# Turning activation tiles through the DMA queue instead of TensorE, in a windowed-attention and mixer kernel

## The chip, the cores and the metric

The kernel runs on one core of a Trainium2 chip. The metric is device time in microseconds (us) of one execution; lower is better. The kernel before took 568.84 us (median of three runs, 568.76 to 569.65).

The engines are named as in the profile: PE is TensorE, DVE is VectorE, ACT is ScalarE, POOL is GpSimd, and SP is SyncE, whose queue issues nearly all transfers.

## The reference, cut to what matters

```
scores = q @ k.T / 8 + bias ; keep = first n_global keys or the last n_local
x  = softmax(scores) @ v                       # 2 x 768 rows, 8 heads x 64 = 512 columns
xn = (x - mean) / sqrt(var + 1e-6) * g_ln      # first mixer layer
x  = x + relu(xn @ w_ch1) @ w_ch2              # 512 -> 2048 -> 512
h  = relu(x.T @ w_tok1) @ w_tok2               # token mixing over 768 rows, per batch
u  = x + h.T
out = u + relu(u @ w_ch1') @ w_ch2'            # 512 -> 1536 -> 512
```

The 1536 rows are twelve tiles T = 0 to 11 of 128 rows, six per batch. Two arrays of activations must be turned (rows to columns) before a product can contract over the 512 columns: the normalised tile `xn` and, after token mixing, the tile `u`, each once per T.

## The kernel before, in words

Products of the mixer run on float16 pairs. A float32 tile is split in a high half (rounded to float16) and a low half (what is left), and a product is three matmuls: high x high, high x low, low x high (`mm3`, lines 372 to 374). So whatever feeds a product is split: ACT writes the high half, then DVE or POOL subtracts it and writes the low half.

The tiles T form four groups of three. Group 0 and 2 are turned into a buffer named `xa`, groups 1 and 3 into `xb`; group 2 reuses the buffer of group 0 when the last product that reads group 0 is done, likewise 3 after 1. The first mixer layer runs as five passes: group 0 with hidden columns 0 and 1 (of four blocks), group 1 the same, then both with block 2, both with block 3, and then groups 2 and 3 together. In that last pass, from its second block on, and in the second channel layer, `mlp_ops` uses a scheme of fewer products with sums of operands (`Factors`, `summands`, tiles `fx`, `sz`, `Q`, `K`, `V`; bank name `chain`). Results of the second product of a layer (`L2`, `L2S`) are added to `x` by DVE at line 872.

Token mixing of batch 0 (T = 0 to 5) is interleaved with the pass of groups 2 and 3, that of batch 1 with the second channel layer of batch 0. Its second product writes `tok`, DVE adds that to `x` (line 1040), and the new tile is turned: T = 0 to 5 into tiles `u`, T = 6 to 11 into `xa` and `xb` again.

Turning, before, is `transpose_ops` (line 558): four matmuls of PE against an identity (line 565) write a PSUM bank, ACT reads the bank and writes the high half (line 358), DVE reads it and writes the low half (line 367). The bank is of pool `k` for `norm` (shared with `chain`) and of pool `t` for `uT` (shared with `L2S`, `T`, `PV` and `tok` of the second product); each pool has two banks.

The order of all instructions is written by a planner (`Plan.order`): every operation has an engine, an assumed duration, a priority from tables of numbers (SLOT, AHEAD, LEAD, DUE and so on), and the planner plays them on a model of the engines. An operation marked `lock` is not started while another locked one of DVE or POOL runs by the model. While group 0 isn't turned, `emit` puts filler matmuls (`keep_busy`, line 106) where the model sees PE idle in its first stretch. SP's queue is in order too: a transfer that waits holds those behind it.

Weights come as 64-bit words: a load into `stg`, ACT makes `fw` (line 727), DVE makes `wf` (line 733), ACT writes the high half (line 749), and POOL (line 752) or DVE (line 755) the low half, of `wa`, `wb` or `t`. Strings such as LOA1 name the engine for each.

Of the kernel before, what the change touches and what calls it, by code (L numbers as in the profile page):

```python
# [17 lines left out]
AF = mybir.ActivationFunctionType  # L18
ALU = mybir.AluOpType
# [549 lines left out]
    plan.op("V", 0.6, prio, l, r=[(b, 0), (*w, "h")], w=[(*w, "l")])  # L569


def xk(T):

    return [("x", T, 0), ("x", T, 1)]


def norm_ops(o, plan, prio, T, grp, i):

    nc = o.nc
    x = o.x[T]  # L580
    st = Buf("st", lambda: o.ln.tile([P, 9], F32, tag="st", name="st", bufs=2))
    xn = Buf("xn", lambda: o.ln.tile([P, C], F32, tag="xn", name="xn", bufs=o.sizes["xn"]))

    def stats():
        nc.vector.bn_stats(out=st.t[:, 0:6], in_=x[:])
        nc.vector.bn_aggr(out=st.t[:, 6:8], in_=st.t[:, 0:6])
        nc.vector.tensor_scalar(out=st.t[:, 8:9], in0=st.t[:, 7:8], scalar1=1e-6, scalar2=None, op0=ALU.add)

    k0 = 4 * T
    op = plan.op  # L590
    op("V", 1.0, prio(k0 + SLOT["st"]), stats, r=xk(T), w=[(st, 0)], get=[st])

# [93 lines left out]
class Weights:  # L686
# [26 lines left out]
    def split(self, src, prio, dst, key, get=(), r=(), after=()):  # L713
        o, nc, op = self.o, self.o.nc, self.plan.op
        wide = o.half and (src[1] == "b" or src[0] == "tok2")
        fine = o.half and not wide
        scale = W3 if fine else W8 if wide and not o.w64 else 1.0
        engs = {(1, "a"): LOA1, (1, "b"): LOB1, (2, "a"): LOA2, (2, "b"): LOB2}.get(src[:2], LOT)
        lo_eng = "V" if scale != 1.0 else engs[src[2]] if o.w64 else "G"
        stg = Buf("stg", lambda: next(o.stg))  # L720
        if o.w64:
            if src in o.staged:
                op("N", max(LOADED[src], HOLD[src[2]]), -9.0 + 0.1 * src[2], lambda: None, w=[(stg, 0)], get=[stg])
            else:
# [24 lines left out]
        op("A", 0.54, prio, lambda: nc.scalar.activation(
            out=dst()[0], in_=shaped(), func=AF.Copy, scale=scale), r=[w, *r], w=[(*key, "h")], get=get, after=after)  # L750
        if lo_eng == "G":
            op("G", 1.26, prio, lambda: nc.gpsimd.tensor_tensor(
                out=dst()[1], in0=shaped(), in1=plain(dst()[0]), op=ALU.subtract), r=[w, (*key, "h"), *r], w=[(*key, "l")], after=after)
        else:
            op("V", 0.6, prio, lambda: nc.vector.scalar_tensor_tensor(
                out=dst()[1], in0=shaped(), scalar=scale, in1=plain(dst()[0]), op0=ALU.mult, op1=ALU.subtract),
               r=[w, (*key, "h"), *r], w=[(*key, "l")], after=after)


def w_view(o, src):  # L760
# [241 lines left out]
def token_ops(o, plan, b, uT, prio):  # L1002
# [27 lines left out]
    for i in range(NT):  # L1030
# [16 lines left out]
AHEAD = {'s': 12.69, 'k': 30.71, 'q': -33.13, 'v': 33.57}  # L1050
STORE, RELOAD = 9.55, -14.48

LOA1 = 'GVGVGVVVGGGVGVVG'
LOB1 = 'GGGVGVGVVGGVGGVG'
LOA2 = 'VGGGGVVGVVVV'
LOB2 = 'GVVVVGVGVGVG'
LOT = 'VVG'
MK0, MK1, MK2 = 'AAVAVVAV', 'AVVAVAAA', 'VVVAAVVA'
HEAD0 = -200.0
MASK2 = 0.1  # L1060
BUSY = 10, 3
HOLD = [-37.47, 19.06, -39.64]
FIRST = [("k", 0), ("q", 0), ("k", 1), ("q", 1), ("v", 0), (1, "a", 0), ("v", 1), (1, "a", 1), ("k", 2), ("q", 2), (1, "a", 2), ("v", 2)]
LOADED = {("k", 0): 0.0, ("q", 0): 0.0, ("k", 1): 0.0, ("q", 1): 0.6, ("v", 0): 1.5, (1, "a", 0): 3.2, ("v", 1): 4.1,
          (1, "a", 1): 5.8, ("k", 2): 6.7, ("q", 2): 7.5, (1, "a", 2): 9.2, ("v", 2): 10.1}
SPLIT = 6
PVE, VCAST = 'AAAVAA', 'AV'
EVX = 'AAAAVVVAAAAV'
# [7 lines left out]
BANKS = {'L1': 'm', 'L2': 'm', 'L2S': 't', 'norm': 'k', 'chain': 'k', 'uT': 't', 'S': 's', 'T': 't', 'PV': 't', 'tok1': 's', 'tok2': 't'}  # L1076
PSUMS = ('m', 's', 't', 'k')
WIDE = {'hid': 5, 'wa': 5, 'wb': 5, 'stg': 3, 'fw': 2, 'wf': 2, 'st': 2, 'xn': 1, 'mn': 3, 'sum': 3, 'ex': 3, 'pt': 2, 'ph': 2, 'pl': 2, 'ao': 2, 'xz': 3, 'sx': 8, 'raw0': 1, 'raw1': 1, 'xa': 1, 'xb': 1, 'm': 2, 'k': 2, 's': 2, 't': 2}
SIZES = {**WIDE, 'hid': 12, 'wa': 8, 'wb': 8, 'wf': 4, 'fw': 3, 'stg': 4, 'xn': 2, 'xz': 3, 'sz': 4}


def store(o, T):
# [24 lines left out]
def rest(o, ctx, attn, fast):  # L1107
# [40 lines left out]
        plan.busy = lambda n: keep_busy(o, idle.t, n)  # L1148
        plan.op("A", 0.55, HEAD0 + 7.5, lambda: [nc.scalar.memzero(y[:]) for y in o.more_fw], w=[("zeros",)])
    attn.ops(o, plan, prio)  # L1150
    last = len(plan.ops)
    for T in range(NTT):
        norm_ops(o, plan, lambda k, T=T: prio(T, k), T, g[of[T][0]], of[T][1])
    if fast:
        plan.op("T", 0.0, 0.0, lambda: setattr(plan, "busy", lambda n: None), r=[(g[0], 1, "h")], w=[(idle, 0)])
    grp = lambda i: (G[i], lambda: g[i].t, gkeys(g[i], n=len(G[i])))
# [41 lines left out]
    for T in range(NTT):  # L1198
        i, j = divmod(T, 3)
        sl = slice(j * P, (j + 1) * P)  # L1200
        if i < 2:
            uT[T] = (lambda i=i, sl=sl: (o.u[i][:, 0, :, sl], o.u[i][:, 1, :, sl])), ("u", i, j), (), ()
        else:
            uT[T] = (lambda i=i, sl=sl: (u[i].t[:, 0, :, sl], u[i].t[:, 1, :, sl])), (u[i], j), ([u[i]] if j == 0 else []), ()
    token_ops(o, plan, 0, uT, lambda n: t - TOK0 + n * (TOK0 - 8) / 26)
    if not fast:
        token_ops(o, plan, 1, uT, lambda n: t - 1 + n * 0.7)
# [38 lines left out]
HEAD = 95.26
DUE = [45.62, 34.37, 67.54, -5.33]
EARLY = [22.25, -19.91, -2.29, -26.75]
LEAD = -124.75
EVAC = 17.45  # L1250
TOK1 = -39.91
TOKW, TOK0 = 143.17, 142.91
# [199 lines left out]
```

## Time and profile before

| what | value |
|---|---|
| median of three runs | 568.84 us |
| profiled execution, its own time | 568.15 us |
| its span | 566.3 us |
| PE busy | 551.8 us (97%) |
| DVE busy | 425.0 us (75%) |
| ACT busy | 333.7 us (59%) |
| POOL busy | 141.3 us (25%) |
| DMA traffic | 80.79 MB, mean 143 GB/s |

The span runs from the first to the last instruction of the program; the device time of the same execution is 1.85 us longer. A busy share is the time in which an engine had an instruction in work; for PE, whose matmuls overlap, the distance between the starts of two matmuls says more than the length of one. The table of stages gives for each stretch the busy time of each engine, the granted TensorE clock (1.00 is full speed) and the share of the sixteen DMA engines.

### The profile page before, as it was taken

To read this page: it belongs to the slowest core of one execution; us is meant where nothing else is said; L and a number is where in the kernel's file an instruction comes from. 1 tells how busy PE (TensorE), PEld (TensorE's weight loads), DVE (VectorE), ACT (ScalarE), POOL (GpSimd) and SP (SyncE) were. 2 spreads that over 40 slices of the span, in tenths; PEclk is the share of its full clock that TensorE was granted. 3 is DMA by queue.
4 is the path that set the end of the run, shared out by engine and by line. 5 is a ranking of instruction groups with operands and counts; after the bars stand their busy time and mean duration, and the time that the engine had idled before them with its cause. 6 is when DMAs were issued, how large, how long until landed. Compare 5 with 4: busy or idle time off the path is not lost.

```text
span 566.3 us, 9485 instructions
## 1 busy us (share of the span) xinstructions
PE 551.8 (97%) x3347; PEld 319.3 (56%) x3347; DVE 425.0 (75%) x939; ACT 333.7 (59%) x750; POOL 141.3 (25%) x153
## 2 busy tenths in 40 slices
PE   8989999999999999999999999998999999999995
PEld 6867767555555765555555555554554555555542
DVE  7888999773766667998867889989858976555431
ACT  6998679783744656557664745767735564534210
POOL 2223345440011223623201142233006122110000
PEclk9999999999999999999999999999899999999999
DMA  8777978887668313027423421473303132302012
GB/s 263 222 242 232 295 220 244 271 274 254 208 211 285 96 34 102 4 70 223 134 76 112 131 74 57 170 247 129 115 12 111 38 130 94 131 0 75 1 39 79
DMA packets 62251, 80.79 MB, mean 143 GB/s; under 512 B 21492, under 2 KB 35828, under 8 KB 62196
## 3 DMA queue, kind: packets, MB, share of 16 engines
q1 hardware_dynamic: 62194, 80.11, 43.9%
q8 instruction: 28, 0.46, 0.3%
q14 instruction: 27, 0.22, 0.1%
q10 hardware_dynamic: 2, 0.00, 0.0%
HBM read 61.87 MB, written 17.83 MB: 141 GB/s over the span
## 4 chain that ended last, share of the span: by engine, by line
PE 75%; DVE 15%; ACT 4%; DMA 2%; issue 2%; POOL 1%; SPq 0%; ACTq 0%; POOLq 0%; DVEq 0%
PE L L372 10%; PE L L374 10%; PE L L373 10%; PE L2S L373 7%; PE L2S L372 7%; PE L2S L374 7%; PE S L453 3%; PE chain L372 3%; PE chain L373 3%; PE T L479 3%; PE chain L374 3%; PE PV L484 3%; DVE x L872 2%; DVE wf L733 2%; DVE Q L806 1%
## 5 line engine op out<-in xcount | busy, mean ns | idle before, releaser
L372 PE MATMUL L2S<-wb,h 128*128 128x512 f16 x228 | 86.4, 379 | 0.0
L373 PE MATMUL L2S<-wb,h 128*128 128x512 f16 x228 | 86.4, 379 | 0.0
L374 PE MATMUL L2S<-wb,h 128*128 128x512 f16 x228 | 86.4, 379 | 0.0
L872 DVE SCALAR_TENSOR_TENSOR x<-L2S,x 128x512 f32<-128x512 f32 x57 | 39.1, 687 | 51.1 <-PE L2S L374 51.0
L727 ACT ACTIVATE fw<-stg 128x512 f16<-128x512 bf16 x62 | 47.6, 778 | 15.5 <-DMA stg<-in_moe_w_ch_dram 8.3
L374 PEld LDWEIGHTS <-h 128*128 128x128 f16 x336 | 32.9, 98 | 39.7
L806 POOL TENSOR_TENSOR Q<-wa 128x512 f32<-128x512 f16 x18 | 26.5, 1471 | 110.0 <-issue 65.2
L372 PEld LDWEIGHTS <-h 128*128 128x128 f16 x336 | 32.9, 98 | 36.7 <-issue 1.0
L373 PEld LDWEIGHTS <-h 128*128 128x128 f16 x336 | 32.9, 98 | 35.6
L474 ACT ACTIVATE ex<-ex,mn 128x256 f32<-128x256 f32 (+1 forms) x96 | 41.0, 483 | 8.6 <-DVE mn L469 8.5
L733 DVE SCALAR_TENSOR_TENSOR wf<-stg,fw 128x512 uint32<-128x512 uint32 x62 | 44.3, 726 | 1.0 <-ACT fw L727 0.8
L372 PE MATMUL L<-wb,h 128*128 128x512 f16 x108 | 41.0, 379 | 0.0
L374 PE MATMUL L<-wb,h 128*128 128x512 f16 x108 | 40.9, 379 | 0.0
L373 PE MATMUL L<-wb,h 128*128 128x512 f16 x108 | 40.9, 379 | 0.0
L372 PEld LDWEIGHTS <-wa 128*128 128x128 f16 x268 | 26.3, 98 | 18.8 <-issue 2.0
L373 PEld LDWEIGHTS <-wa 128*128 128x128 f16 x268 | 26.2, 98 | 17.7 <-issue 0.9
L374 PEld LDWEIGHTS <-wa 128*128 128x128 f16 x268 | 26.2, 98 | 17.3
L364 DVE SCALAR_TENSOR_TENSOR h<-L,h 128x384 f16<-128x384 f32 x40 | 22.1, 551 | 18.0 <-ACT h L358 17.9
L358 ACT ACTIVATE h<-L 128x384 f16<-128x384 f32 x40 | 19.5, 488 | 26.4 <-PE L L374 26.0
L372 PE MATMUL L<-xa,wa 128*128 128x384 f16 x104 | 33.9, 326 | 0.1
L374 PE MATMUL L<-xa,wa 128*128 128x384 f16 x104 | 33.9, 326 | 0.0
L373 PE MATMUL L<-xa,wa 128*128 128x384 f16 x104 | 33.9, 326 | 0.0
(241 smaller groups left out, 1412.1 us busy)
## 6 DMA issues: line engine op xcount, KB each, us to landing
stg<-in_moe_w_ch_dram SPq DMA_DIRECT2D x56, 512.0 KB, 4.7
wa<-scr_1a SPq DMA_DIRECT2D x24, 256.0 KB, 3.7
wb<-scr_1b SPq DMA_DIRECT2D x24, 256.0 KB, 3.7
scr_1a<-wa SPq DMA_DIRECT2D x16, 256.0 KB, 5.0
scr_1b<-wb SPq DMA_DIRECT2D x16, 256.0 KB, 3.3
K<-in_k_dram SPq DMA_DIRECT2D x12, 256.0 KB, 3.4
Q<-in_q_dram SPq DMA_DIRECT2D x12, 256.0 KB, 4.2
V<-in_v_dram SPq DMA_DIRECT2D x12, 256.0 KB, 3.8
```

The source lines that it names most:

```text
L358: nc.scalar.activation(out=hi(), in_=src(), func=AF.Relu if relu else AF.Copy)
L364: nc.vector.scalar_tensor_tensor(out=lo(), in0=src(), scalar=0.0, in1=plain(hi()), op0=ALU.max, op1=ALU.subtract)
L372: nc.tensor.matmul(ps, ah, bh, start=first, stop=False, **k)
L373: nc.tensor.matmul(ps, ah, bl, start=False, stop=False, **k)
L374: nc.tensor.matmul(ps, al, bh, start=False, stop=last, **k)
L453: nc.tensor.matmul(bs[j].t[:, i, :w], o.Q[r, qs, p + i, :], o.K[r, slots, p + i, :], start=True, stop=True)
L474: nc.scalar.activation(out=ex.t[:, j, :w], in_=ex.t[:, j, :w], func=AF.Exp, bias=mn.t[:, h:h + 1], scale=-1.0)
L479: nc.tensor.transpose(bt.t[:, j, i, :], ex.t[:, j, i * P:(i + 1) * P], o.ident[:])
L727: op("A", 0.66, prio - 2, lambda: nc.scalar.activation(out=fw.t[:, :, 1], in_=stg.t[:, 4:2049:4].bitcast(BF16), func=AF.Copy, scale=2.0 if ...
L733: op("V", 0.6, prio - 1, lambda: nc.vector.scalar_tensor_tensor(out=raw().bitcast(U32), in0=stg.t.bitcast(U32)[:, 1:1024:2], scalar=13, in ...
L806: op(eng, {"G": 0.1 + n * 0.00227, "V": 0.07 + n * 0.00104}[eng], prio, lambda: e.tensor_tensor(out=out(), in0=a(), in1=b(), op=alu), lock ...
L872: n = op("V", 0.6, prio, lambda: nc.vector.scalar_tensor_tensor(out=x[:], in0=b.t[:], scalar=BACK if o.half else 1.0, in1=x[:], op0=ALU.mu ...
```

## The change

Only the fast float16 branch changes. Where a tile is turned, `turn_ops` stands in place of `transpose_ops`: ACT copies the float32 tile in SBUF to the high half of a new tile `xh`, DVE or POOL (strings NLO and ULO) subtracts and writes the low half beside it, and one DMA on SP's queue (`transpose=True`) turns the 128 x 1024 float16 numbers of both halves into the destination. `xh` and `uh` have two buffers each. The planner is given TURN = 2.5 us for that DMA. The low half of a weight on DVE (line 755) gets `lock=True`. The tables of the planner have other numbers, and some engine strings differ. The operations of the norm tiles now also stand ahead of the point at which the attention's buffers are given up (`last`), since they use its pool.

```diff
+def turn_ops(o, plan, prio, pool, tag, lo_eng, src, r, dst, w, get=()):
+    nc, op = o.nc, plan.op
+    y = Buf(tag, lambda: pool().tile([P, 2, C], F16, tag=tag, name="xh", bufs=o.sizes[tag]))
+    op("A", 0.52, prio, lambda: nc.scalar.activation(out=y.t[:, 0], in_=src(), func=AF.Copy), r=r, w=[(y, "h")], get=[y])
+    e = {"V": nc.vector, "G": nc.gpsimd}[lo_eng]
+    op(lo_eng, {"V": 0.6, "G": 1.26}[lo_eng], prio, lambda: e.tensor_tensor(out=y.t[:, 1], in0=src(), in1=y.t[:, 0], op=ALU.subtract),
+       r=[*r, (y, "h")], w=[(y, "l")], lock=True)
+    op("S", TURN, prio, lambda: nc.sync.dma_start(dst().rearrange("p s k n -> p (s k) n"), y.t[:].rearrange("p s c -> p (s c)"), transpose=True),
+       r=[(y, "h"), (y, "l")], w=[(*w, "h"), (*w, "l")], get=get)
...
+    if o.half:
+        turn_ops(o, plan, prio(k0 + SLOT["tr"]), lambda: ln, "xh", NLO[T], lambda: xn.t[:], [(xn, 0)], lambda: grp.t[:, :, :, sl],
+                 (grp, i), [grp] if i == 0 else [])
+        return
     transpose_ops(o, plan, prio(k0 + SLOT["tr"]), "norm", lambda: xn.t, [(xn, 0)], lambda: (grp.t[:, 0, :, sl], grp.t[:, 1, :, sl]),
...
-               r=[w, (*key, "h"), *r], w=[(*key, "l")], after=after)
+               r=[w, (*key, "h"), *r], w=[(*key, "l")], after=after, lock=True)
...
+        if o.half:
+            turn_ops(o, plan, prio(14 + 2 * i) - (1 - b) * UP, lambda: o.tk, "uh", ULO[T], lambda T=T: o.x[T][:], [*xk(T), ("tk",), *r], dst, key, get)
+            continue
...
-LOT = 'VVG'
+LOT = 'VGG'
+NLO, ULO = 'GGVGGGGGVVGV', 'VGVVVGVGGVVG'
+TURN = 2.5
+UP = 19.85
...
-FE, SE = 'VGGVVVVGVVVV', 'VGVVGVVV'
+FE, SE = 'VVGVGGGGVVGG', 'VGVVVVGV'
```

Counted in the fast branch, the changed program has 96 fewer transposing matmuls (48 `norm`, 48 `uT`), 16 more fillers on PE (51 in place of 35 of `L<-x`), 30 fewer instructions on DVE, 3 fewer on ACT, 32 more on POOL, and 24 more transfers on SP's queue. The other PE instructions are the same in number.

Three places show the order. The first is PE in the head of the program, from the second half of the products with V of T = 2 to the first product of the mixer (`L<-xa`), before:

```order
L484 MATMUL PV<-V,pt 128x65 x8
L479 MATMUL T<-ident,ex 128x128 x4
L453 MATMUL S<-K,Q 128x256 x4
L479 MATMUL T<-ident,ex 128x128 x4
L484 MATMUL PV<-V,pt 128x65 x8
L479 MATMUL T<-ident,ex 128x128 x4
L565 MATMUL norm<-ident,xn 128x128 x4
L479 MATMUL T<-ident,ex 128x128 x4
L453 MATMUL S<-K,Q 128x256 x4
L484 MATMUL PV<-V,pt 128x65 x8
L372 LDWEIGHTS wa
L372 MATMUL L_766<-xa,wa 128x384
```

The same place now:

```order
L484 MATMUL PV<-V,pt 128x65 x8
L479 MATMUL T<-ident,ex 128x128 x4
L453 MATMUL S<-K,Q 128x256 x4
L479 MATMUL T<-ident,ex 128x128 x4
L484 MATMUL PV<-V,pt 128x65 x8
L479 MATMUL T<-ident,ex 128x128 x4
L453 MATMUL S<-K,Q 128x256 x4
L479 MATMUL T<-ident,ex 128x128 x4
L484 MATMUL PV<-V,pt 128x65 x8
L479 MATMUL T<-ident,ex 128x128 x4
L453 MATMUL S<-K,Q 128x256 x4
L479 MATMUL T<-ident,ex 128x128 x4
```

The turn of T = 2 (`norm`) is gone from PE, and one more step of the attention (`S`) with two more `T` stands ahead of the first `L<-xa`, which follows directly on the last row. A row of `S` or `PV` with x4 or x8 is eight or sixteen matmuls in the trace, since a float32 one is recorded twice there.

The second place is SP's queue in the head, with the first transfer that turns a tile (T = 0) and what stands behind it, now:

```order
L580 DMA_TRANSPOSE xa<-xh 128x8x128
L537 DMA V<-in_v_dram 32x8x64
L158 DMA V<-in_v_dram 128x8x64
L535 DMA K<-in_k_dram 128x4x32
L160 DMA K<-in_k_dram 128x512
L160 DMA Q<-in_q_dram 128x512
L725 DMA scr_1a_583<-wa 128x1024
L580 DMA_TRANSPOSE xa<-xh 128x8x128
```

Loads of the next attention tiles are queued behind each turn; before, no such transfer stood between them.

The third place is DVE at the start of the second token product of batch 1 (`z<-tok`, then `x<-tok`), before:

```order
L364 SCALAR_TENSOR_TENSOR z<-tok_4409,z 128x512
L364 SCALAR_TENSOR_TENSOR z<-tok_4410,z 128x512
L806 TENSOR_TENSOR Q<-Q 128x256
L733 SCALAR_TENSOR_TENSOR wf<-stg,fw_62 128x512
L755 SCALAR_TENSOR_TENSOR wa<-wf,wa 128x512
L733 SCALAR_TENSOR_TENSOR wf<-stg,fw_63 128x512
L872 SCALAR_TENSOR_TENSOR x_65<-L2S,x_65 128x512
```

The same place now:

```order
L364 SCALAR_TENSOR_TENSOR z<-tok_4483,z 128x512
L364 SCALAR_TENSOR_TENSOR z<-tok_4484,z 128x512
L823 TENSOR_TENSOR Q<-wa 128x512
L772 SCALAR_TENSOR_TENSOR wa<-wf,wa 128x512
L750 SCALAR_TENSOR_TENSOR wf<-stg_203,fw_204 128x512
L889 SCALAR_TENSOR_TENSOR x_68<-L2S,x_68 128x512
```

Between `z` and the operation that empties an `L2S` bank stood four operations, now three.

## Rows read from the trace of the kernel before

**Rows 1.** The page: busy us of each engine, share, instructions; granted clock by slices.

```profile
PE 551.8 (97%) x3347; PEld 319.3 (56%) x3347; DVE 425.0 (75%) x939; ACT 333.7 (59%) x750; POOL 141.3 (25%) x153
...
PEclk9999999999999999999999999999899999999999
```

**Rows 2.** Chain that ended last: start us, us until the next piece, what.

```profile
13.38 0.55 PE L L106 x5
...
20.30 1.06 PE S L453 x8
...
21.95 1.85 PE PV L484 x16
23.81 0.44 PE norm L565 x4
...
28.84 0.44 PE T L479 x4
...
400.64 0.87 PE uT L565 x8
...
403.46 0.22 PE tok L372
```

**Rows 3.** Groups of PE by line and form: busy us, mean ns; idle before.

```profile
L565 PE MATMUL uT<-ident,x 128*128 128x128 f32 x48 | 7.0, 273 | 0.0
L565 PE MATMUL norm<-ident,xn 128*128 128x128 f32 x48 | 6.9, 273 | 0.0
```

**Rows 4.** PE in time order, head: start us, us, instruction; idle before it, releaser.

```profile
31.60 1.90 PE L484 MATMUL PV<-V,pt 128*128 128x65 f32 x16
...
38.53 1.11 PE L484 MATMUL PV<-V,pt 128*128 128x65 f32 x8 [1.22 <-ACT pt L515]
...
44.11 0.33 PE L372 MATMUL L<-xa,wa 128*128 128x384 f16 x1
...
46.06 0.60 PE L479 MATMUL T<-ident,ex 128*128 128x128 f32 x4
```

**Rows 5.** POOL and DVE in time order: T = 2 from normalised to turned.

```profile
38.08 1.34 POOL L607 TENSOR_TENSOR xn<-xn,gB 128x512 f32<-128x512 f32 x1 [0.93 <-ACT xn L600]
...
41.63 0.69 DVE L367 TENSOR_TENSOR xa<-norm,xa 128x512 f16<-128x512 f32 x1
```

**Rows 6.** DMA issues on the page: KB each, median us from issue to landing.

```profile
wa<-scr_1a SPq DMA_DIRECT2D x24, 256.0 KB, 3.7
...
stg<-in_moe_w_tok_dram SPq DMA_DIRECT2D x6, 512.0 KB, 6.2
...
vb<-vb SPq DMA_DIRECT2D x4, 97.5 KB, 2.2
```

**Rows 7.** Stages: us; PE, PEld, DVE, ACT, POOL busy; PEclk, DMA share, GB/s.

```profile
0.00:100.00 100.00, 94.87 (x732) 71.47 (x733) 87.32 (x303) 80.68 (x184) 34.24 (x64) 1.00 0.80 244
393.00:396.30 3.30, 1.10 (x6) 0.39 (x4) 3.30 (x6) 1.43 (x3) 1.04 (x1) 1.00 0.49 171
396.30:400.00 3.70, 3.39 (x10) 1.29 (x10) 3.02 (x6) 1.39 (x3) 0.00 (x0) 0.54 0.42 147
```

**Rows 8.** All engines in time order around PE's longest wait.

```profile
392.01 1.28 DVE L364 SCALAR_TENSOR_TENSOR z<-tok,z 128x512 f16<-128x512 f32 x2
...
393.76 1.04 POOL L806 TENSOR_TENSOR Q<-Q 128x256 f32<-128x256 f32 x1 [4.83 <-DVE Q L806]
394.14 1.21 DVE L755 SCALAR_TENSOR_TENSOR wa<-wf,wa 128x512 f16<-128x512 f32 x1
...
395.88 0.68 DVE L872 SCALAR_TENSOR_TENSOR x<-L2S,x 128x512 f32<-128x512 f32 x1
...
396.61 0.59 PE L372 MATMUL tok<-z,t 128*128 128x512 f16 x1 [2.50 <-DVE x L872]
...
397.84 0.63 PE L372 MATMUL tok<-z,t 128*128 128x512 f16 x1
```

**Rows 9.** One tile's instructions, `wf`: ns shortest, median, longest; first and last start.

```profile
L755 DVE SCALAR_TENSOR_TENSOR wa<-wf,wa x28: 679/691/1646, 21.3 to 396.8; 128x512 f16<-128x512 f32 x28
```

More of the change, by code (lines that the diff above doesn't have):

```diff
@@ L580, in norm_ops @@
     x = o.x[T]
-    st = Buf("st", lambda: o.ln.tile([P, 9], F32, tag="st", name="st", bufs=2))
-    xn = Buf("xn", lambda: o.ln.tile([P, C], F32, tag="xn", name="xn", bufs=o.sizes["xn"]))
+    ln = o.sm if o.half else o.ln
+    st = Buf("st", lambda: ln.tile([P, 9], F32, tag="st", name="st", bufs=2))
+    xn = Buf("xn", lambda: ln.tile([P, C], F32, tag="xn", name="xn", bufs=o.sizes["xn"]))
     def stats():
@@ L1044, in token_ops @@
         dst, key, get, r = uT[T]
+        if o.half:
+            turn_ops(o, plan, prio(14 + 2 * i) - (1 - b) * UP, lambda: o.tk, "uh", ULO[T], lambda T=T: o.x[T][:], [*xk(T), ("tk",), *r], dst, key, get)
+            continue
         transpose_ops(o, plan, prio(14 + 2 * i), "uT", lambda T=T: o.x[T][:], [*xk(T), ("tk",), *r], dst, key, get)
[L1050 to L1056, printed above, removed]
-LOT = 'VVG'
-MK0, MK1, MK2 = 'AAVAVVAV', 'AVVAVAAA', 'VVVAAVVA'
+AHEAD = {'s': -8.81, 'k': 53.46, 'q': -8.16, 'v': 42.47}
+STORE, RELOAD = 53.17, 7.48
+LOA1 = 'GVGGVVVVVGGVVGVV'
+LOB1 = 'GGGGVGVGVGVVGVVV'
+LOA2 = 'GGGVVVVVVGVG'
+LOB2 = 'VVVVVVGVVVGV'
+LOT = 'VGG'
+NLO, ULO = 'GGVGGGGGVVGV', 'VGVVVGVGGVVG'
+TURN = 2.5
+UP = 19.85
+MK0, MK1, MK2 = 'VVVVAAAA', 'VAVVAAAA', 'AVVVAVAA'
 HEAD0 = -200.0
-MASK2 = 0.1
+MASK2 = -121.51
 BUSY = 10, 3
-HOLD = [-37.47, 19.06, -39.64]
+HOLD = [-39.73, 27.18, 27.27]
 FIRST = [("k", 0), ("q", 0), ("k", 1), ("q", 1), ("v", 0), (1, "a", 0), ("v", 1), (1, "a", 1), ("k", 2), ("q", 2), (1, "a", 2), ("v", 2)]
@@ L1066 @@
 SPLIT = 6
-PVE, VCAST = 'AAAVAA', 'AV'
-EVX = 'AAAAVVVAAAAV'
+PVE, VCAST = 'AAAAVV', 'VA'
+EVX = 'AAVAAVVVVAAV'
 QKC, PVC = 0.266, 0.224
-SLOT = {'gk': -57.12, 'exp': 54.15, 'T': -29.6, 'PV': 0.2, 'inv': -1.8, 'st': 27.26, 'xn': 4.52, 'tr': 4.36}
+SLOT = {'gk': -69.67, 'exp': 60.81, 'T': -40.62, 'PV': -12.2, 'inv': 18.38, 'st': 39.04, 'xn': 13.67, 'tr': 37.13}
 NACT = range(0, 4)
@@ L1078 @@
 WIDE = {'hid': 5, 'wa': 5, 'wb': 5, 'stg': 3, 'fw': 2, 'wf': 2, 'st': 2, 'xn': 1, 'mn': 3, 'sum': 3, 'ex': 3, 'pt': 2, 'ph': 2, 'pl': 2, 'ao': 2, 'xz': 3, 'sx': 8, 'raw0': 1, 'raw1': 1, 'xa': 1, 'xb': 1, 'm': 2, 'k': 2, 's': 2, 't': 2}
-SIZES = {**WIDE, 'hid': 12, 'wa': 8, 'wb': 8, 'wf': 4, 'fw': 3, 'stg': 4, 'xn': 2, 'xz': 3, 'sz': 4}
+SIZES = {**WIDE, 'hid': 12, 'wa': 8, 'wb': 8, 'wf': 4, 'fw': 3, 'stg': 4, 'xn': 2, 'xh': 2, 'uh': 2, 'xz': 3, 'sz': 4}
 def store(o, T):
@@ L1150, in rest @@
     attn.ops(o, plan, prio)
-    last = len(plan.ops)
     for T in range(NTT):
         norm_ops(o, plan, lambda k, T=T: prio(T, k), T, g[of[T][0]], of[T][1])
+    last = len(plan.ops)
     if fast:
@@ L1201, in rest @@
         if i < 2:
-            uT[T] = (lambda i=i, sl=sl: (o.u[i][:, 0, :, sl], o.u[i][:, 1, :, sl])), ("u", i, j), (), ()
+            dst, key, get = (lambda i=i, sl=sl: o.u[i][:, :, :, sl]), ("u", i, j), ()
         else:
-            uT[T] = (lambda i=i, sl=sl: (u[i].t[:, 0, :, sl], u[i].t[:, 1, :, sl])), (u[i], j), ([u[i]] if j == 0 else []), ()
+            dst, key, get = (lambda i=i, sl=sl: u[i].t[:, :, :, sl]), (u[i], j), ([u[i]] if j == 0 else [])
+        uT[T] = (dst if fast else lambda dst=dst: (dst()[:, 0], dst()[:, 1])), key, get, ()
     token_ops(o, plan, 0, uT, lambda n: t - TOK0 + n * (TOK0 - 8) / 26)
@@ L1242 @@
 BLOCKS2 = [[(c, (0, 1)) for c in range(3)]] * 2
-LEADS, FLEAD = -62.8, 212.9
-F2LEAD = [-38.18, -45.25]
-FE, SE = 'VGGVVVVGVVVV', 'VGVVGVVV'
[L1246 to L1252, printed above, removed]
+LEADS, FLEAD = -12.39, 152.38
+F2LEAD = [-40.38, -38.53]
+FE, SE = 'VVGVGGGGVVGG', 'VGVVVVGV'
+HEAD = 85.06
+DUE = [36.2, 20.0, 77.7, 9.05]
+EARLY = [6.29, -8.69, 7.57, -14.12]
+LEAD = -208.54
+EVAC = 35.43
+TOK1 = 41.27
+TOKW, TOK0 = 191.94, 141.69
 SLOW = dict(SLOT={'gk': -30.97, 'exp': 16.12, 'T': -15.37, 'PV': -13.48, 'inv': 9.01, 'st': 17.62, 'xn': 12.62, 'tr': 1.7}, HEAD=107.54, DUE=[32.9, 21.07, 45.09, 4.38], EARLY=[-15.89, -16.66, 3.92, -16.37], LEAD=21.63, EVAC=3.31,
```

## The prediction

> **What bounds the kernel now.** I read the page first: PE is busy for 551.8 of 566.3 us, DVE for 75% [rows 1]. A busy PE is not by itself a bound, so the second view is the chain that ended last, whose times are from start to start: four transposing matmuls take 0.44 us, a 512-column matmul 0.22, five fillers 0.55, all one behind the other with no gap [rows 2]. The reader is to see that PE runs at its own pace for almost the whole span, and that what is taken off PE comes off the time, unless a wait takes its place. Third, the waits: PE's longest is 2.50 us, before the second `tok` product of batch 1, for a DVE operation; right behind it the granted clock is 0.54 over 3.7 us, at 1.00 before, so the slower of the two levels (1.2 GHz in place of 2.4) for most of that stretch [rows 7, 8]. It is the one slice short of a 9 in the page's clock row, and shorter waits, as that of 1.22 us in the head, left it at 9 [rows 1, 4]. Last, the stage of the first 100 us: PE 94.9, DVE 87.3, ACT 80.7, DMA engines 0.80 [rows 7]. Everything is nearly full there, and it is where a new wait would hurt.
>
> **The change part by part.** The sum is made against the profiled execution's own 568.15 us, which is 0.69 below the median of 568.84; differences are taken over to the median unchanged.
>
> *Turns off PE.* 24 turns of four matmuls (48 `norm` and 48 `uT` [rows 3]), each four worth 0.44 us: 24 x 0.44 = 10.6, by the eight of 0.87 us 12 x 0.87 = 10.4 [rows 2]. I take 10.5. All of it is on the path as long as PE is the bound. -10.5.
>
> *Fillers.* 16 more of 0.11 us [rows 2]: 1.76. They stand where the planner expects PE idle in the head; if PE would wait there anyhow they are free. From 0 to 1.76; I take +1.7, since with PE on the path they delay what follows.
>
> *What ACT, DVE and POOL do in place of it.* ACT has 3 instructions fewer, DVE 30 fewer, POOL 32 more. POOL is busy for 25% of the span [rows 1], so it has room; DVE gets lighter. No cost; and the gain stands only in the item on the wait below.
>
> *The transfer that turns a tile.* The trace before has none. It moves 256 KB from SBUF to SBUF. Nearest rows, from issue to landing: a 97.5 KB copy inside SBUF 2.2 us, a 256 KB reload 3.7, a 512 KB load 6.2 [rows 6]. For the low end 2.2, for the high end twice the slowest row, 12.4, because no row excludes that a turn in eight blocks is slow; I take the row of the same size, 3.7 (L below).
> Where does L count? First the head, T = 2. Before, its `PV` ends at 33.50, `xn` at 39.42, the turned tile stands at 42.32 and the first `L<-xa` starts at 44.11, so PE came last, not the tile [rows 4, 5]. After the same `PV`, PE now has six `T` (0.44), three `S` (1.06) and two `PV` (1.85): 9.5 us; before four `T`, one `norm`, two `S` and two `PV`: 8.0, while 10.6 passed, so 2.6 went in waits such as that of 1.22 [rows 2, 4]. The tile needs 5.9 us to `xn`, then a copy and a subtraction at about 0.7 each (as the subtraction before [rows 5]) with some queueing, 2.1 together, then L: 8.0 + L. PE is there after 9.5 (no waits) to 12.1 (the same waits). At L = 3.7 the tile comes at 11.7: a wait from 0 to 2.2; at 6.2, from 2.1 to 4.7. I take +0.8. The 1.5 us of attention that now stand ahead of the first product are not lost.
> Second, the hand-over of `xa` to group 2 and of `xb` to group 3, where the destination is only free after the last product that reads the old group. In the new order PE has, between the last `L<-xa` of group 0 and the first of group 2, 48 matmuls of 384 columns (twelve take 1.95, so 0.163 each [rows 4]), 36 of 512 at 0.216 and some small ones: 16.9 us; for `xb`, 48 and 36 without the small ones: 15.6. The third tile of a group must wait for a buffer of `xh`: two turns in a row and 1.6 us between, 2L + 1.6, so 9.0 at 3.7 and 14.0 at 6.2. Hidden; it begins to cost at L = 7. Third, token mixing: between its last product and the first that reads the turned tiles stand 22.8 us (batch 0) and 29.3 (batch 1), counted in the same way, and no L up to 12.4 gets through that alone. On SP's queue loads of Q, K, V stand behind each turn, as behind a store of weights before; the planner puts the turn where its source is due. +0.8 for all of this.
>
> *The wait at 396 us.* DVE ends `z` at 393.29 and empties the `L2S` bank only at 396.56, with four operations between; one of them, `wa`, took 1.21 where its shortest is 0.68, beside a POOL operation that ran from 393.76 to 394.80 [rows 8, 9]. That form is the one that the planner now keeps apart from POOL's. In the new order three operations stand there, 3 x 0.68 and 0.68 for the emptying: the bank is free 2.7 us behind `z`. PE first has one `tok` product, 6 x 0.216, and now also six 384-column matmuls, 0.98: 2.3. So the wait goes from 2.5 to about 0.5, and the slow stretch, six `tok` matmuls and some more at double length, goes with it: of 3.7 us at 0.54, 3.7 x 0.46 = 1.7 us are lost there [rows 7, 8]. From 0 (DVE comes late again) to -4.2; I take -2.0 - 1.7 = -3.7.
>
> Sum: -10.5 + 1.7 + 0.8 - 3.7 = -11.7, and 568.84 - 11.7 = 557.1 us.
>
> A rule of the Trainium skill speaks against the change: "VectorE: DVE Perf Modes", Rules for kernel authors, says to turn 128x128 on TensorE if a result in PSUM is acceptable and by the DMA crossbar otherwise; its table in The three transpose paths gives 390 ns for the one and 1309 ns for the other. Here four turns of PE took 0.44 us from start to start [rows 2], below that page's figure; eight blocks one behind another at its DMA figure would be an estimate of L of 10.5 us, and the sum would be that of the slow rival below. Another page, "Advanced Engine Details and Errata", X-Bar Transpose (TRN2), has such transfers as fast as others, and by that the sum stands. No row here decides between them.
>
> **The rivals.**
> *A wait takes the place.* The wait at 396 moves and doesn't go (3.7 is not gained), and about 2 us of new ones come in, in the order that all tables changed: 557.1 + 3.7 + 2 = 563. For it: DVE is full around 396 [rows 7], and the head has 2.6 us of such waits. Against: DVE has less to do.
> *The turns are slow, and it gets slower.* One mechanism: L decides over the head (8.0 + L against 10.8, the middle of PE's two times) and over the two hand-overs (2L + 1.6 against 16.9 and 15.6). Beyond L = 8 these cost (L - 2.8) + (2L - 15.3) + (2L - 14) = 5L - 32.1; the gain of 12.5 without the 0.8 is eaten at L = 8.9. At L = 10 they cost 17.9, and the time is 568.84 - 12.5 + 17.9 = 574. For it: the DMA engines are at 0.80 in the head [rows 7], where six of the turns stand. Against: no transfer of 256 KB on the page lands later than in 6.
> *It doesn't do what it says.* PE's turns lay in time that was idle anyhow. Then only the other terms stay, with the cover they lose: 568. Against: the turns start without idle time before them [rows 3].
>
> **How the numbers follow.** Forecast 0.55 (its own range 554 to 561: fillers free and the wait wholly gone at the low end, nothing of the wait gained at the high one); a wait in its place 0.22; slow turns 0.13; no effect 0.05; still faster, below 554, because a lighter DVE also shortens the head's waits, 0.05. The range 552.5 to 566 leaves out the slow turns and part of the rest. A measurement of this kernel can tell 0.2% (1.1 us) from no change. Faster: 0.55 + 0.22 + 0.05 = 0.82; same 0.05; slower 0.13.
>
> **What would show it.** PE's busy time about 9 us lower, no `norm` and `uT`, and DVE below 425 us. The landing of the turns between 2.2 and 6.2 us. The first `L<-xa` between 43 and 48 us. No slice of the clock row below 9 near 390. No wait of PE over 1 us at the first product of group 2 or 3. It is wrong if a turn lands later than 9 us, if PE waits for `xa` or `xb`, or if PE's idle time grows by what its busy time falls.

## The result and the profile after

The changed kernel takes 554.67 us (median of four runs, 554.48 to 554.81); the kernel before took 568.80 beside it. The ratio is 0.9749 [0.9732, 0.9766], a gain of 14.1 us where 11.7 were forecast. The profiled execution took 554.65 us with a span of 552.9. Measured again, beside the last experiments (c1), the ratio was 0.9777 [0.9751, 0.9803], a gain of 12.5.

The page of the changed kernel, in the form of [rows 1]: busy time, share and instructions of each engine, then the granted clock.

```profile
PE 543.2 (98%) x3267; PEld 310.7 (56%) x3267; DVE 408.9 (74%) x909; ACT 334.9 (61%) x747; POOL 178.0 (32%) x185
...
PEclk9999999999999999999999999999999999999998
```

PE is busy for 8.6 us less and idle for 9.7 us (552.9 - 543.2) in place of 14.5 (566.3 - 551.8), so 4.8 less: together the 13.4 us by which the span fell. The slice below 9 near 396 us is gone (the 8 of the last slice lies at the end, where PE has no work left). Where the idle time went is seen by stages. First the kernel before, with the columns of [rows 7] (the stage 0 to 100 stands there):

```profile
200.00:300.00 100.00, 99.28 (x583) 55.08 (x582) 81.55 (x152) 62.56 (x147) 29.32 (x25) 1.00 0.29 90
300.00:400.00 100.00, 97.50 (x509) 50.12 (x507) 89.31 (x153) 61.12 (x131) 27.27 (x20) 0.98 0.39 135
```

And the changed kernel, the same stages, the head and a stretch within it:

```profile
0.00:100.00 100.00, 96.52 (x723) 71.87 (x724) 80.97 (x286) 78.41 (x176) 41.78 (x70) 0.98 0.82 229
40.50:43.90 3.40, 3.40 (x16) 2.56 (x16) 2.46 (x6) 2.85 (x6) 0.14 (x1) 0.50 0.72 230
200.00:300.00 100.00, 100.00 (x533) 51.86 (x532) 72.88 (x126) 61.64 (x144) 35.65 (x31) 1.00 0.52 135
300.00:400.00 100.00, 100.00 (x529) 51.61 (x528) 88.96 (x153) 63.71 (x133) 34.80 (x29) 1.00 0.43 130
```

PE is never idle from 200 to 400 us now: 0.72 + 2.50 = 3.2 us of idle time are gone there, and 1.65 in the first 100 us (94.87 to 96.52), where DVE fell from 87.3 to 81.0. The clock is not at 1.00 all the way: in the profiled execution a stretch at 0.50 (the lower of the two levels) lies at 40.5 us, as long as the one that was at 396. The idle time of the first 100 us is not steady either: the second profile of the same kernel (c1) has no such stretch there and is 0.3 us above the kernel before, not 1.65.

```profile
0.00:100.00 100.00, 95.19 (x718) 70.42 (x719) 80.41 (x286) 77.65 (x175) 41.20 (x69) 1.00 0.84 229
```

The turns themselves, all instructions of the line that issues them: duration on SP's queue in ns (shortest, median, longest), first and last start, and the time from issue to landing in us.

```profile
L580 SPq DMA_TRANSPOSE xa<-xh x9: 1232/1283/1445, 23.1 to 412.5; - x9
L580 SPq DMA_TRANSPOSE xb<-xh x9: 1232/1238/1289, 54.4 to 428.4; - x9
L580 SPq DMA_TRANSPOSE u<-xh x6: 1233/1238/1260, 267.3 to 320.7; - x6
...
DMA to landing us min/median/max: 3.0/3.2/6.2
```

A turn holds SP's queue for 1.24 us and lands after 3.2 us; the prediction had taken 3.7. In the head, in order of time (start, us, engine, line; idle time before and its releaser):

```profile
39.37 1.27 POOL L620 TENSOR_TENSOR xn<-xn,gB 128x512 f32<-128x512 f32 x1 [0.93 <-ACT xn L613]
...
39.74 0.84 PE L479 MATMUL T<-ident,ex 128*128 128x128 f32 x4 [0.40 <-ACT ex L474]
...
42.16 1.28 SPq L580 DMA_TRANSPOSE xa<-xh  x1
...
46.21 0.44 PE L479 MATMUL T<-ident,ex 128*128 128x128 f32 x2 [0.44 <-ACT ex L474]
...
48.38 0.33 PE L372 MATMUL L<-xa,wa 128*128 128x384 f16 x1
```

These answer to [rows 4, 5]. The tile of T = 2 stands at about 45.3 (42.16, and 3.1 for the landing of this transfer) and PE starts the first `L<-xa` at 48.38 with no idle time before it: the turn is hidden. Last, the place of [rows 8], now at 398 us:

```profile
398.17 1.27 DVE L364 SCALAR_TENSOR_TENSOR z<-tok,z 128x512 f16<-128x512 f32 x2
...
399.97 0.68 DVE L772 SCALAR_TENSOR_TENSOR wa<-wf,wa 128x512 f16<-128x512 f32 x1
...
401.17 0.68 DVE L889 SCALAR_TENSOR_TENSOR x<-L2S,x 128x512 f32<-128x512 f32 x1
...
402.92 0.38 PE L372 MATMUL tok<-z,t 128*128 128x512 f16 x1
```

`wa` takes 0.68 us where it took 1.21, DVE empties the bank at 401.85, and PE needs it only at 402.92, with no wait.

### The profile page after: what moved, and what is told of

Same layout as the page of the kernel before. It is cut to its first block, busy times and chain, and to the rows that moved or that the text cites. A ratio compares the mean times of both kernels' runs of the same rounds, so it can differ in the third digit from the quotient of the medians.

```text
span 552.9 us, 9384 instructions
## 1 busy us (share of the span) xinstructions
PE 543.2 (98%) x3267; PEld 310.7 (56%) x3267; DVE 408.9 (74%) x909; ACT 334.9 (61%) x747; POOL 178.0 (32%) x185
## 4 chain that ended last, share of the span: by engine, by line
PE 94%; DVE 2%; ACT 2%; issue 1%; POOL 0%; POOLq 0%; ACTq 0%
PE L L372 12%; PE L L374 12%; PE L L373 12%; PE L2S L374 9%; PE L2S L373 9%; PE L2S L372 9%; PE chain L372 4%; PE chain L374 4%; PE chain L373 4%; PE S L453 4%; PE T L479 3%; PE PV L484 2%; PE tok L374 2%; PE tok L372 2%; PE tok L373 2%
## 5 line engine op out<-in xcount | busy, mean ns | idle before, releaser
L744 ACT ACTIVATE fw<-stg 128x512 f16<-128x512 bf16 x62 | 48.0, 776 | 10.5 <-DMA stg<-in_moe_w_ch_dram 7.2
L474 ACT ACTIVATE ex<-ex,mn 128x256 f32<-128x256 f32 (+1 forms) x96 | 41.6, 480 | 14.1 <-DVE mn L469 13.9
L823 POOL TENSOR_TENSOR sz<-Q,sz 128x512 f16<-128x512 f32 x18 | 22.4, 1242 | 84.6 <-ACT sz L915 84.6
L889 DVE SCALAR_TENSOR_TENSOR x<-L,x 128x512 f32<-128x512 f32 x27 | 18.6, 690 | 22.2 <-PE L L374 22.1
L372 PE MATMUL L<-xa,wa 128*128 128x384 f16 x104 | 34.0, 326 | 0.0
L373 PE MATMUL L<-xa,wa 128*128 128x384 f16 x104 | 33.9, 326 | 0.0
```

What stands on the lines that cost most here:

```text
L372: nc.tensor.matmul(ps, ah, bh, start=first, stop=False, **k)
L373: nc.tensor.matmul(ps, ah, bl, start=False, stop=False, **k)
L474: nc.scalar.activation(out=ex.t[:, j, :w], in_=ex.t[:, j, :w], func=AF.Exp, bias=mn.t[:, h:h + 1], scale=-1.0)
L744: op("A", 0.66, prio - 2, lambda: nc.scalar.activation(out=fw.t[:, :, 1], in_=stg.t[:, 4:2049:4].bitcast(BF16), func=AF.Copy, scale=2.0 if ...
L823: op(eng, {"G": 0.1 + n * 0.00227, "V": 0.07 + n * 0.00104}[eng], prio, lambda: e.tensor_tensor(out=out(), in0=a(), in1=b(), op=alu), lock ...
L889: n = op("V", 0.6, prio, lambda: nc.vector.scalar_tensor_tensor(out=x[:], in0=b.t[:], scalar=BACK if o.half else 1.0, in1=x[:], op0=ALU.mu ...
```

## The experiments

Runs of one table ran on the same chip beside the kernel before. Since the time before differs a little from chip to chip, ratios are compared across tables.

**Code, tables and lock apart.** Three edits come together in the change: the turns, the `lock` on a weight's low half, and new numbers in the planner's tables. Four kernels split them.

| run | ratio to before, 95% | median us (before 567.50) |
|---|---|---|
| a1: turns and lock, old tables | 0.9919 [0.9893, 0.9946] | 564.01 |
| a2: lock and new tables, turns on PE | 0.9932 [0.9910, 0.9953] | 563.57 |
| a3: lock alone | 0.9946 [0.9924, 0.9968] | 564.02 |
| a4: all but the lock | 0.9815 [0.9770, 0.9861] | 557.68 |

*a1*, the changed kernel with the tables of before (those of the turns kept; the same for the tables not shown):

```diff
-SLOT = {'gk': -69.67, 'exp': 60.81, 'T': -40.62, 'PV': -12.2, 'inv': 18.38, 'st': 39.04, 'xn': 13.67, 'tr': 37.13}
+SLOT = {'gk': -57.12, 'exp': 54.15, 'T': -29.6, 'PV': 0.2, 'inv': -1.8, 'st': 27.26, 'xn': 4.52, 'tr': 4.36}
...
-LEAD = -208.54
+LEAD = -124.75
```

> The changed code with the planner's tables of numbers of the kernel before (the lock on the weights' low half stays in, since without it the planner finds no order). Theory PE: what the turns take off PE, 10.5 us, comes off the time whatever the tables; with new waits in an order that was not made for them, 558 to 562. Theory order: the new tables bring most of it; then this stays at 565 or more.

*a2*, the kernel before with the lock and the new tables; `norm` is turned on PE, and its `tr` entry is set to that of `xn`:

```diff
-SLOT = {'gk': -57.12, 'exp': 54.15, 'T': -29.6, 'PV': 0.2, 'inv': -1.8, 'st': 27.26, 'xn': 4.52, 'tr': 4.36}
+SLOT = {'gk': -69.67, 'exp': 60.81, 'T': -40.62, 'PV': -12.2, 'inv': 18.38, 'st': 39.04, 'xn': 13.67, 'tr': 13.67}
...
-LEAD = -124.75
+LEAD = -208.54
...
-               r=[w, (*key, "h"), *r], w=[(*key, "l")], after=after)
+               r=[w, (*key, "h"), *r], w=[(*key, "l")], after=after, lock=True)
```

> The code of before with the lock and with the new tables (one number, the place of the turn of a normalised tile, moved earlier, since the planner finds no order with it), turns on PE. Theory PE: 565 to 572, since PE has the same work as before. Theory order: 560 or less.

*a3*, the kernel before with that last line alone:

> The kernel before with the lock alone. If the collision of DVE and POOL makes the 2.5 us wait at 396 us and the half clock behind it, 564.5 to 566; if that wait comes from the order on DVE, 568 to 570.

*a4*, the changed kernel without it:

> The changed kernel without the lock, all else the same. Theory PE: 554.5 to 556.5, as DVE has room; if the lock matters, 558 or more, with a wait of PE for DVE of 2 us or more somewhere from 200 to 430 us.

Taken to the 568.80 us of the result by their ratios, the four are 564.2, 564.9, 565.7 and 558.3 us. So a1 falls between its two theories, a2 just under that of PE, and a3 into the range of the collision; a4 falls into the range in which the lock matters, but without the wait that was named for it (below).

a3: the lock alone gains 0.54%, 3.1 us. Its clock row and two stages:

```profile
PEclk9999999999999999999999999999999999999999
...
200.00:300.00 100.00, 100.00 (x590) 55.77 (x589) 83.01 (x157) 64.19 (x152) 27.59 (x25) 1.00 0.29 90
300.00:400.00 100.00, 100.00 (x536) 52.70 (x535) 86.44 (x156) 63.06 (x137) 25.54 (x20) 1.00 0.39 131
```

Idle time of 2.5 us and the slow stretch are both gone, by one edit of the planner's rules and with every turn still on PE; so are the 0.72 us from 200 to 300, with DVE at 83.01, above the 81.55 of before. But the edit changes the order too. DVE by itself, at the place of [rows 8] in a3:

```profile
388.00 1.29 DVE L364 SCALAR_TENSOR_TENSOR z<-tok,z 128x512 f16<-128x512 f32 x2 [0.64 <-ACT z L360]
389.21 0.42 DVE L806 TENSOR_TENSOR Q<-Q 128x256 f32<-128x256 f32 x1
389.54 0.68 DVE L733 SCALAR_TENSOR_TENSOR wf<-stg,fw 128x512 uint32<-128x512 uint32 x1
390.14 0.69 DVE L872 SCALAR_TENSOR_TENSOR x<-L2S,x 128x512 f32<-128x512 f32 x1
```

Between `z` and the emptying of the bank stand two operations in place of four, and `wa` is not one of them: the bank is free 1.5 us behind `z`, where it was 3.3. So the lock takes the wait away; whether by a shorter `wa` or by the order that it leads to, a3 does not part. And the lock is not needed for it in the new order: in a4, PE waits at this place for 0.29 us.

```profile
405.88 0.38 PE L372 MATMUL tok<-z,t 128*128 128x512 f16 x1 [0.29 <-DVE x L889]
```

Most of what a4 loses lies in the first 100 us, where PE is busy for 93.69 us in its profile (the slowest of its four runs, 559.54), with waits of 2.5 us in all for ACT's `ex` and 1.8 for its `pt`.

What the lock does to the locked form is seen in `wa` of the kernel after and of a4 (ns shortest, median, longest). The changed kernel:

```profile
L772 DVE SCALAR_TENSOR_TENSOR wa<-wf,wa x28: 676/682/1143, 23.3 to 400.0; 128x512 f16<-128x512 f32 x28
```

And without the lock:

```profile
L772 DVE SCALAR_TENSOR_TENSOR wa<-wf,wa x28: 676/684/1641, 23.4 to 401.4; 128x512 f16<-128x512 f32 x28
```

The longest falls by 0.5 us and the median stays; before it was 1646 [rows 9]. In a3 one `wb` of the locked form still takes 1643 ns, so not every long one goes. The Trainium skill, "SBUF — State Buffer", section Who interferes with whom, says that a VectorE instruction with two SBUF inputs contends with a GpSimd instruction that reads SBUF, through a port that they share. The rows agree in kind, with up to about 1 us added to a 0.68 us operation; that it is this port no run shows by itself.

a1 and a3 together: with the old tables the turns add only 0.27% to the lock, less than the intervals tell apart. a2 and a3: the new tables alone add 0.14%, nothing that can be told. All three together give 2.2 to 2.5%. So the 10.5 us of the turns did not come in the order of before, and came in an order made for them. A part of what a1 lost is seen in its trace. SP's queue, POOL and PE in the head of a1:

```profile
32.06 1.16 POOL L578 TENSOR_TENSOR xh<-xn,xh 128x512 f16<-128x512 f32 x1 [1.85 <-ACT xh L576]
...
33.25 1.24 SPq L580 DMA_TRANSPOSE xa<-xh  x1
34.59 1.18 SPq L537 DMA_DIRECT2D V<-in_v_dram  x1
...
36.47 0.63 SPq L158 DMA_DIRECT2D V<-in_v_dram  x1
...
39.21 1.99 PE L484 MATMUL PV<-V,pt 128*128 128x65 f32 x14 [2.69 <-DMA V<-in_v_dram]
```

The load of V stands behind a turn that waits for its source (POOL writes the low half until 33.22), and PE stands 2.69 us for V. With two waits of 1.7 and 1.0 us for DVE later on, and a clock of 0.98 in the first 100 us, PE's idle time is 559.5 - 543.3 = 16.2 us, more than the 14.5 of before. This run took 561.25 us, less than the median of 564.01; what the slower ones lost beyond it, no trace shows.

**How PE and SP set the time.** Four variants of the changed kernel.

| run | ratio to before, 95% | median us (before 566.57) |
|---|---|---|
| b1: each turn as eight transfers | 1.2278 [1.2246, 1.2311] | 694.83 |
| b2: each turn as two transfers | 0.9787 [0.9768, 0.9806] | 554.53 |
| b3: 48 more matmuls on PE | 0.9975 [0.9961, 0.9989] | 564.76 |
| b4: 25 more fillers in the head | 0.9792 [0.9767, 0.9816] | 554.54 |

*b1* (for *b2*, 4 blocks each and `range(2)`):

```diff
-    op("S", TURN, prio, lambda: nc.sync.dma_start(dst().rearrange("p s k n -> p (s k) n"), y.t[:].rearrange("p s c -> p (s c)"), transpose=True),
+    op("S", TURN, prio, lambda: [nc.sync.dma_start(dst().rearrange("p s k n -> p (s k) n")[:, 1 * j:1 * j + 1], y.t[:].rearrange("p s c -> p (s c)")[:, 1 * P * j:1 * P * (j + 1)], transpose=True) for j in range(8)],
```

> Each turn as eight transfers of one 128 x 128 block in place of one, the order of everything else the same. With eight issues of about 1.2 us one behind another a tile lands after 10 to 13 us. Theory L (the prediction's formula, 5L - 32 beyond 8 us): 575 to 585. Rival: the queue behind the turns, not the turned tile, then decides (24 x 8.7 us more on SP), and PE waits for weights as well: 590 or more. If the issue time goes by blocks and not by transfers, 556 or less.

> Each turn as two transfers (high half, low half). A tile lands after 4 to 5 us. Theory L: at most 1.5 us in the head, 554.7 to 556.2. If the head is already waiting for the turned tile, a full 1 us or more: 556 or more.

*b3*, 48 matmuls of 512 columns whose results are overwritten, ahead of second products of the layers (from 72 to 498 us in its trace):

```diff
+            o.seen = getattr(o, "seen", 0) + (mine[0] == 0)
...
+                for _ in range(2 if i == 0 and o.half and o.seen % 3 == 1 and o.seen < 72 else 0):
+                    nc.tensor.matmul(b.t[:], h[:, 0, sl], w[:, 0, :], start=True, stop=True)
```

> The changed kernel with 48 more 512-column matmuls on PE, two ahead of every third second product (24 places), 48 x 0.216 = 10.4 us, their result overwritten. Theory PE: 554.7 + 10.4 = 565.1 (within 1 us). If part of PE's time is slack, 562 or less.

*b4*, fillers for a longer stretch, until the turn of T = 2 (76 in place of 51):

```diff
-        plan.WARM = (1, 8)
+        plan.WARM = (1, 15)
...
-        plan.op("T", 0.0, 0.0, lambda: setattr(plan, "busy", lambda n: None), r=[(g[0], 1, "h")], w=[(idle, 0)])
+        plan.op("T", 0.0, 0.0, lambda: setattr(plan, "busy", lambda n: None), r=[(g[0], 2, "h")], w=[(idle, 0)])
```

> The changed kernel with 25 more fillers in the head, up to 46 us by the planner and until T = 2 is turned. In the changed kernel's trace the granted clock is at half from 40.5 to 43.9 us, behind waits of PE at 39 and 40 us: 1.7 us lost. If fillers keep it at full and lie in waits: 553. If they only stand in the way: 554.7 + 25 x 0.11 = 557.4.

The changed kernel itself has no run beside these, so b2, which should take the same time, stands for it. b3 against b2: 48 x 0.216 = 10.4 us put on PE, 10.2 us more time. There PE is the bound, one to one. b4 against b2: 25 x 0.11 = 2.75 us of fillers cost nothing; they fill time in which PE would wait. Nor does a stretch at half clock in the head cost anything that can be told: in the profile of b4 the clock is at 1.00 through the first 100 us, and the 553 us that this was to bring did not come.

b1 went far beyond what was priced for slow turns; the queue, the rival of its expectation (590 or more), decides. Its transfers, in the view of the line that issues them:

```profile
L580 SPq DMA_TRANSPOSE xa<-xh x72: 1093/1230/2244, 22.0 to 540.1; - x72
...
DMA to landing us min/median/max: 2.2/2.4/7.6
```

A transfer of an eighth of the size holds SP just as long, 1.23 us; a tile is complete after 8 x 1.23 and 1.2 more for the last landing, 11 us. Two places of b1 in order of time, around its two longest waits of PE:

```profile
274.71 0.43 SPq L166 DMA_DIRECT2D stg<-in_moe_w_ch_dram  x1
275.24 20.68 SPq L580 DMA_TRANSPOSE xb<-xh  x16
...
297.32 1.67 ACT L358 ACTIVATE xs<-x 128x512 f16<-128x512 f32 x3 [17.46 <-DMA xb<-xh]
...
299.40 0.56 DVE L364 SCALAR_TENSOR_TENSOR h<-L,h 128x384 f16<-128x384 f32 x1 [5.54 <-ACT h L358]
...
300.01 0.48 PE L372 MATMUL L<-xb,wa 128*128 128x384 f16 x1 [16.77 <-DVE h L364]
...
383.45 10.11 SPq L580 DMA_TRANSPOSE u<-xh  x8
393.66 0.52 SPq L715 DMA_DIRECT2D wa<-scr_1a  x1
...
396.61 0.63 ACT L671 ACTIVATE junk<-wa 128x512 bf16<-128x512 f16 x1 [14.15 <-DMA wa<-scr_1a]
...
403.35 0.48 PE L372 MATMUL chain<-fx,sz 128*128 128x384 f16 x1 [14.17 <-ACT K L945]
```

At the first, ACT stands 17.5 us for turns and PE waits behind it, by way of DVE. At the second a load of weights is issued only after the 10 us of a turn, ACT stands 14.2 us for it, and PE waits for ACT's `K`, which is queued behind. So SP and ACT, both in order, hand the delay to work that has nothing to do with the turn. In all 192 transfers keep SP for 236 us, and the clock over the span is 0.911. In b2, 48 transfers of 1.21 us take 58 us of SP and cost nothing yet.

**Parts of the turns, the planner's cost of one, and the fillers.**

| run | ratio to before, 95% | median us (before 567.55) |
|---|---|---|
| c1: the changed kernel again | 0.9777 [0.9751, 0.9803] | 555.04 |
| c2: only `norm` turned by transfer | 0.9863 [0.9841, 0.9886] | 559.87 |
| c3: TURN 1.4 | 0.9805 [0.9773, 0.9838] | 555.93 |
| c4: no fillers | 0.9879 [0.9840, 0.9918] | 560.52 |

c2 (which also hands over the destination of `uT` as two halves again), c3 and c4, each by itself:

```diff
-        if o.half:
+        if False:
             turn_ops(o, plan, prio(14 + 2 * i) - (1 - b) * UP, lambda: o.tk, "uh", ULO[T], lambda T=T: o.x[T][:], [*xk(T), ("tk",), *r], dst, key, get)
...
-TURN = 2.5
+TURN = 1.4
...
-        plan.busy = lambda n: keep_busy(o, idle.t, n)
+        plan.busy = lambda n: None
```

> The changed kernel once more, beside the others of this chip. Both theories: ratio to the kernel before 0.973 to 0.979 (0.9749 was measured). It is the base for the three runs below.

> Changed kernel, only the twelve norm tiles turned by transfer; the twelve uT turns back on TensorE (48 matmuls, 12 x 0.44 = 5.3 us of PE). Theory 'PE is the bound, each turn taken off it comes off the time': changed kernel + 5.3, ratio to it 1.0095 (1.007 to 1.012). Rival 'the numbers in the tables decide, turns are worth what the order lets them': uT's bank and DVE's reads come back where the tables no longer provide for them, + 8 to + 14 us, ratio 1.014 to 1.025; or, if the uT turns were beside idle time, + 0 to 2.

> Changed kernel with TURN = 1.4 in place of 2.5 in the planner's model (a transfer occupied SP for 1.24 us). Theory 'PE is the bound and nearly full': nothing to win beyond the 16.8 us by which PE's starts lag now, of which most is in the head; - 2 to + 2 us. Rival 'the tables fit one order, any other number shuffles it': slower by 3 to 8 us, with waits of over 1 us on PE that the changed kernel doesn't have.

> Changed kernel without the filler matmuls of the head (51 of 0.11 us = 5.6 us of PE). Theory 'fillers stand on the path, as the sum took the 16 added ones': 4 to 5.6 us faster unless the clock falls. Rival 'they stand where PE would wait anyhow' (25 more cost nothing): same within 1 us, idle time in the head in their place; and if the granted clock then is at 0.5 for longer in the head, slower by half of that stretch, + 1 to + 6.

c2: twelve turns back on PE cost 4.8 us (559.87 - 555.04), where 12 x 0.44 = 5.3 were counted. Its busy row beside that of c1; c1 first:

```profile
PE 542.5 (98%) x3267; PEld 309.8 (56%) x3267; DVE 409.0 (74%) x909; ACT 334.8 (60%) x747; POOL 177.9 (32%) x185
```

Then c2:

```profile
PE 547.9 (98%) x3315; PEld 315.3 (56%) x3315; DVE 408.9 (73%) x914; ACT 333.8 (60%) x747; POOL 171.7 (31%) x180
```

PE's busy time rises by 5.4 us for 48 matmuls. The table theory's 8 to 14 us is ruled out for these tiles. c3: a transfer cost nearer to the 1.24 us that SP shows gives no better order; its six runs spread over 4.8 us and the interval overlaps that of c1.

c4 is a miss of the theory that fillers stand on the path: without them it is 5.5 us slower, not 4 to 5.6 faster. PE waits of c4 (engine, line, for what; us in total, times, longest), the profiled run at 557.3:

```profile
PE T L479 <- ACT ex L474: 3.7, 6, 1.7
...
PE PV L484 <- ACT pt L515: 0.9, 1, 0.9
```

The first 100 us have 92.1 us of PE in place of 95.2 in c1, so 3.1 us more idle time for 5.6 us less work, and the clock is 0.91 from 20 to 40 us. The order of other engines changed with them. The six runs spread from 556.7 to 564.1, and their granted clocks, 0.994 to 0.998, do not go with their times (the slowest has 0.998). A clock of 0.91 over 20 us is 1.8 us lost, so the clock is at most a part of the 5.5; how the order makes the rest stays open. None of the variants beats the changed kernel.

## Why the prediction was right, step by step

*Turns off PE, -10.5.* Right. The page's busy time of PE fell by 8.6 = 10.5 less 1.7 of fillers, within 0.2; c2 gives back half of it. Without the turns the new order is at 0.9932 (a2), with them at 0.9749 to 0.9777: 8.8 to 10.4 us. That they came off the path whole is due to the tables too, which the prediction took as given, with no term for it: with the old ones the turns brought some 1.5 us (a1 beside a3), and the forecast would have been 7 us short of the time (564.2 beside 557.1). To that extent the number was lucky.

*Fillers, +1.7.* Mis-sized: 0. They are in PE's busy time, but 25 more took no time (b4), and without any the kernel was slower (c4).

*The transfer's latency, +0.8.* L was 3.2 at the median and the tile came 3 us before PE wanted it, so 0. PE itself was later than the 43 to 48 us expected (48.38), by two waits of 0.4 for ACT's `ex` and a stretch at half clock. There is no wait of PE for a turned tile. The figure of the Trainium skill that spoke against the change, in "VectorE: DVE Perf Modes", The three transpose paths, 1309 ns for a 128x128 block, gives an estimate of 10.5 us for eight blocks, one behind the other; the trace has 3.2 for all eight in one transfer, and 2.4 for a block alone (b1). What the Trainium skill says in "Advanced Engine Details and Errata", X-Bar Transpose (TRN2), that these transfers are as fast as others, agrees in landing: 3.2 us beside 3.7 for a reload of the same size [rows 6]. In time on the DMA engines it does not: 2.0 us beside 0.8 (last section).

*The wait at 396 us, -3.7.* The wait went wholly (-2.5 where -2.0 stood). The cause named, the unlocked form beside POOL, is shown only as far as the edit goes: the lock alone takes the wait away (a3), but its order changed there as well, and in the new order the wait is down to 0.29 us without the lock (a4). The half clock behind the wait, -1.7, went from that place to the head, where it costs nothing that can be told: the profiles of c1, b2 and b4 have no such stretch before the end, and their spans are 553.6, 552.8 and 552.3 us beside the 552.9 with it. All that the lock brings by itself is -3.1 (a3).

*What the sum came to.* With what runs measured in time for each term it is -9.7 for the turns (twice the 4.8 of c2), 0 for the fillers, 0 for the latency and -3.1 for the lock: -12.8, between the 12.5 and the 14.1 measured for the whole. Each of these differences is known to one or two us only. The two terms that were priced and cost nothing, +1.7 and +0.8, are the clear part of the 2.4 us by which the forecast fell short. 554.67 is the low end of the forecast's own range, which stood for just that: fillers free and the wait wholly gone. The 0.72 us of idle time from 200 to 300 us, which the sum had not counted, go with the lock too (a3).

*The rivals.* A wait in its place: excluded, since idle time fell. No effect: excluded by c2, where half of the turns give back 4.8 us. Still faster, by a lighter DVE that shortens the head's waits: not shown. The time is not below 554, the 1.65 us of the first 100 are 0.3 in c1, and the idle time from 200 to 300 went in a3 with DVE as full as before. Slow turns: L = 3.2 excludes them, but b1 shows that the rival was priced by the wrong resource. Its formula, 5L - 32.1, gives 23 us for a tile that is complete after some 11 us (8 x 1.23, and 1.2 for the last landing); b1 lost 140 (694.8 - 554.5). The prediction had passed over SP's queue with a sentence (loads stand behind each turn as behind a store), which holds at 1.24 us a turn and not at 10, and over ACT's order altogether.

## What to carry to other kernels

Where the chain of waits is one engine end to end, what leaves that engine comes off the time one to one, unless a wait takes its place (a1); check it by adding work of known size (b3). Price a transfer twice, by when it lands and by how long it holds the queue that issues it, and turn a tile in one transfer, not in eight. When code and an order written by numbers change together, try the code in the old order and the order with the old code: here each was worth a third of a per cent or less beyond the lock, and both together 1.7 to 2.0. A rule of a planner that keeps two operations apart also moves others: look at the order at the place before naming the cause (a3).

## What the runs showed of the hardware

The hold of a turning transfer on SP does not depend on its size, from one block to eight: 1.23 us for one (b1), 1.21 for four (b2), 1.24 to 1.28 for eight, at the median, while most plain transfers beside it take 0.33 to 0.7. Landing grows slowly: 2.4, 2.8 and 3.2 us at the median.

A turn is dear in engine time, though not late. The page's counts for the kernel before:

```profile
DMA packets 62251, 80.79 MB, mean 143 GB/s; under 512 B 21492, under 2 KB 35828, under 8 KB 62196
...
q1 hardware_dynamic: 62194, 80.11, 43.9%
```

And for the changed kernel:

```profile
DMA packets 87596, 87.09 MB, mean 158 GB/s; under 512 B 46836, under 2 KB 61172, under 8 KB 87540
...
q1 hardware_dynamic: 87538, 86.40, 53.6%
```

The 25344 small packets more are 1056 for each of 24 turns, and 0.536 x 552.9 - 0.439 x 566.3 = 47.8 us of all sixteen engines, 2.0 us a turn if all of it is put down to the turns (c1 and c2, twelve turns apart, give 1.75). The transfers of before took 0.8 us for as many bytes (0.439 x 566.3 us for 80.11 MB). No cost of this shows in the time; the DMA share of the first 100 us went from 0.80 to 0.82.
